# Layer 2's first token group runs its down projection in seven products, and layer 1's activation ends in PSUM

## The chip, the cores and the metric

One core of a Trainium2 chip runs the whole program. The metric is device time in microseconds (us), the median of the runs of one kernel. TensorE is called PE here, VectorE DVE, ScalarE ACT, GpSimd POOL; SP (SyncE) issues the DMAs.

## The reference

Attention with rotary embedding over 4 x 8 heads of 576 tokens and 64 features, then two feed-forward layers over 2304 tokens, d_model 512 and d_ff 2048, all in float32:

```python
x = attn_out.transpose(0, 2, 1, 3).reshape(2304, 512)
h = x @ moe_w_in;  x = (h - np.tanh(h)) @ moe_w_out                  # layer 1
h = x @ moe2_w_in; out = (h / (1.0 + np.exp(-1.702 * h))) @ moe2_w_out   # layer 2
```

The inputs of the two layers come as raw 8-byte words of which the kernel makes float32 weights.

## The kernel before

**Precision.** A float32 product is made of three fast ones: every operand is split into a rounded high part (ACT, a cast) and a low part (value minus high part, POOL or DVE), and high*high, high*low and low*high are added in PSUM.

**Layer 1** has 96 items, one for each of six blocks of 384 tokens and sixteen feature rows of 128 (`item_ops`, `act`, `split`). An item is twelve up matmuls (`up`, L836), the activation, the split of its result, and twelve down matmuls (`down`, L941). The activation g = h - tanh(h) works like this: ACT squares h into z (L901), takes tanh into t (L903), squares z again into u, which lies in PSUM (L906), and makes the mask mk from z (L908). DVE makes w from z and h (L910), subtracts t = h - t (L912), puts a polynomial for small h together in u (L914, L916), and copies u into t where the mask says so (`copy_predicated`, L918). ACT casts t to the high part gh (L926), and POOL makes the low part gl = t - gh (L928), which the down matmuls wait for. h lies in one of the PSUM banks b0 and b1, u in b2, and the raw words that are being converted (`cp`, L325) in b3. w, t, mk and z are SBUF tiles.

Beside the items POOL, ACT and DVE convert weights (`Conv`): the bits (POOL L334, DVE L336), then split parts. For layer 2 they make sums of quarter blocks as well (`conv_in`), split these too (`pieces_of`: ACT L381, POOL L384) and store them to the DRAM tiles w2 (L387). `conv_out` does one word of w_out at a time, without sums.

**Layer 2** takes the six blocks in three pairs (p = 0, 1, 2, the groups) and the sixteen feature rows in eight pairs: 24 steps q (`quad_ops`). A step's up projection is seven products of half-size blocks in place of eight (`product`, L1138, 42 matmuls of 384 columns). The down projection of groups 1 and 2 is seven products too (`down_ops`, `dprod`, L1265): POOL adds and subtracts the four g blocks (L1234 to L1241), seven operands are split (L1397, L1400), 63 matmuls of 256 columns follow, and DVE or ACT adds their results to sums in SBUF (`drain`, L1296 to L1300). The last step of such a group can't be done so and uses `last_down` (L1322, 72 matmuls of 256 columns); then the sums are joined and stored (`close` L1306, `final` L1328, `final_save` L1338). Group 0 runs its down projection plainly (`down2`, L1179, 36 matmuls of 512 columns a step) and meanwhile makes the turned w_out blocks that groups 1 and 2 need (`turn_ops`, ten operations and one store a step, L1198 to L1215).

**What sets the order.** Every operation is given to a planner (`Plan`) with a priority, its cost on each engine that may run it, and the buffers that it uses. The planner lays them out in time and gives each engine a fixed order of instructions; an engine then runs them in that order, each as soon as what it waits for is there. `port=True` tells the planner that an operation on DVE can't run beside POOL; the five DVE operations of layer 1's activation don't carry it. SP issues all DMAs in its own fixed order.

## Time and profile before

| what | us |
|---|---|
| median of 3 runs (1063.17 to 1063.38) | 1063.25 |
| the profiled execution | 1063.46 |
| its span, from the first to the last instruction | 1061.7 |
| PE busy with matmuls | 1038.3 (98%) |
| DVE busy | 693.8 (65%) |
| ACT busy | 719.7 (68%) |
| POOL busy | 780.1 (73%) |
| granted TensorE clock, mean | 0.999 |

Attention lasts to 282 us, layer 1 to 681, the three groups of layer 2 to 805, 926 and the end. A matmul's record is longer than the time it adds to PE, since matmuls overlap: twelve of 384 columns take 2.08 us. So the time from a run of matmuls to the same run one step on is the thing to read.

### The profile page before, as it was taken

To read this page: it belongs to the slowest core of one execution; us is meant where nothing else is said; L and a number is where in the kernel's file an instruction comes from. 1 tells how busy PE (TensorE), PEld (TensorE's weight loads), DVE (VectorE), ACT (ScalarE), POOL (GpSimd) and SP (SyncE) were. 2 spreads that over 40 slices of the span, in tenths; PEclk is the share of its full clock that TensorE was granted. 3 is DMA by queue.
4 is the path that set the end of the run, shared out by engine and by line. 5 is a ranking of instruction groups with operands and counts; after the bars stand their busy time and mean duration, and the time that the engine had idled before them with its cause. 6 is when DMAs were issued, how large, how long until landed. Compare 5 with 4: busy or idle time off the path is not lost.

```text
span 1061.7 us, 19352 instructions
## 1 busy us (share of the span) xinstructions
PE 1038.3 (98%) x6578; PEld 998.7 (94%) x6578; DVE 693.8 (65%) x1243; ACT 719.7 (68%) x1623; POOL 780.1 (73%) x667
## 2 busy tenths in 40 slices
PE   5999999999999999999999999999999999999998
PEld 3898899998999999999999999998888999999998
DVE  7899898899787887777677776654121333562335
ACT  5999999989887776667767776743545444544442
POOL 2888899989356669869978868933933779977763
PEclk9999999999999999999999999999999999999999
DMA  8868778768433326655756578487468676777621
GB/s 280 281 237 308 260 277 281 259 224 294 152 99 120 105 96 214 209 193 191 243 189 227 189 259 308 156 308 280 157 221 340 233 291 224 263 283 266 232 99 60
DMA packets 107188, 236.36 MB, mean 223 GB/s; under 512 B 11729, under 2 KB 61137, under 8 KB 100049
## 3 DMA queue, kind: packets, MB, share of 16 engines
q1 hardware_dynamic: 107088, 235.12, 63.8%
q8 instruction: 52, 0.85, 0.3%
q14 instruction: 48, 0.39, 0.1%
HBM read 157.42 MB, written 49.36 MB: 195 GB/s over the span
## 4 chain that ended last, share of the span: by engine, by line
PE 77%; DVE 7%; ACT 5%; POOL 4%; DMA 3%; issue 3%; SPq 1%; DVEq 0%; ACTq 0%; POOLq 0%
PE ps_h L836 18%; PE y L941 18%; PE ps_h L1138 17%; PE y L1265 10%; PE y L1179 6%; DVE mx L567 2%; PE sp L561 2%; DVE el L624 2%; ACT e L573 2%; PE ps_o L640 2%; PE y L1322 2%; POOL qk L484 1%; PE ps_e L598 1%; ACT eh L626 1%; DMA st<-in_moe_w_out_dram 1%
## 5 line engine op out<-in xcount | busy, mean ns | idle before, releaser
L836 PE MATMUL ps_h<-xh,w 128*128 128x384 f32 x768 | 210.8, 336 | 0.2 <-ACT u L906 0.2
L1138 PE MATMUL ps_h<-xo,ws 128*128 128x384 f32 x1008 | 201.3, 341 | 0.0
L941 PE MATMUL y<-gh,w 128*128 128x384 f32 x768 | 195.6, 336 | 0.0
L1138 PEld LDWEIGHTS ps_h<-xo,ws 128*128 128x128 f32 x1008 | 173.5, 188 | 8.1 <-ACT su L1148 2.1
L836 PEld LDWEIGHTS ps_h<-xh,w 128*128 128x128 f32 x768 | 140.1, 188 | 0.7 <-ACT u L906 0.5
L941 PEld LDWEIGHTS y<-gh,w 128*128 128x128 f32 x768 | 139.0, 188 | 0.0
L928 POOL TENSOR_TENSOR gl<-t,gh 128x384 fp32r<-128x384 f32 x96 | 97.8, 1019 | 42.7 <-ACT gh L926 33.9
L941 PE MATMUL y<-gl,w 128*128 128x384 f32 x384 | 129.0, 336 | 0.0
L836 PE MATMUL ps_h<-xl,w 128*128 128x384 f32 x384 | 128.8, 335 | 0.0
L1296 DVE TENSOR_TENSOR sum<-y,sum 128x256 f32<-128x256 f32 (+1 forms) x108 | 54.0, 537 | 112.8 <-PE y L1265 112.8
L561 PE MATMUL sp<-kt,qt 128*128 128x288 f32 x624 | 115.8, 313 | 1.5 <-ACT e L573 0.9
L573 ACT ACTIVATE e<-sp,mx 128x576 f32<-128x576 f32 x144 | 107.5, 747 | 12.8 <-DVE mx L567 11.6
L567 DVE TENSOR_REDUCE mx<-sp 128x1 f32<-128x576 f32 x144 | 107.2, 748 | 4.8 <-PE sp L561 3.2
L624 DVE TENSOR_TENSOR el<-ps_e,eh 128x512 fp32r<-128x512 f32 x144 | 96.5, 684 | 14.3 <-ACT eh L626 13.4
L626 ACT CAST eh<-ps_e 128x512 fp32r<-128x512 f32 (+2 forms) x208 | 101.7, 532 | 4.6 <-PE ps_e L602 2.0
L910 DVE SCALAR_TENSOR_TENSOR w<-z,ps_h 128x384 f32<-128x384 f32 x96 | 52.8, 550 | 78.5 <-ACT t L903 78.2
L926 ACT CAST gh<-t 128x384 fp32r<-128x384 f32 x96 | 49.3, 513 | 70.9 <-DVE t L918 60.7
L561 PEld LDWEIGHTS sp<-kt,qt 128*128 128x128 f32 x624 | 87.9, 189 | 9.1 <-ACT e L573 7.7
L640 PE MATMUL ps_o<-eh,vw 128*128 128x256 f32 (+1 forms) x320 | 91.1, 307 | 3.5 <-DVE el L624 2.6
L1400 POOL TENSOR_TENSOR ex<-t,g2h 128x384 fp32r<-128x384 f32 x72 | 72.2, 1019 | 25.3 <-ACT g2h L1397 25.3
L1265 PE MATMUL y<-ws,g2h 128*128 128x256 f32 x486 | 90.1, 283 | 0.0
L1265 PE MATMUL y<-ws,ex 128*128 128x256 f32 x345 | 80.7, 282 | 0.0
(143 smaller groups left out, 2525.0 us busy)
## 6 DMA issues: line engine op xcount, KB each, us to landing
ws<-w SPq DMA_DIRECT2D x48, 1024.0 KB
w<-part SPq DMA_DIRECT2D x40, 512.0 KB
kt<-qk SPq DMA_DIRECT2D x64, 288.0 KB
ws<-w SPq DMA_DIRECT2D x24, 768.0 KB
qk<-in_qk_dram SPq DMA_DIRECT2D x30, 576.0 KB
st<-in_moe_w_in_dram SPq DMA_DIRECT2D x32, 512.0 KB
st<-in_moe_w_out_dram SPq DMA_DIRECT2D x32, 512.0 KB
qt<-qk SPq DMA_DIRECT2D x64, 144.0 KB
```

Source lines behind the costliest of these rows:

```text
L561: nc.tensor.matmul(sp[:, half, 0:HS], lhsT=w, rhs=m[:, half * HS:(half + 1) * HS], start=(o == 0), stop=(o == len(ops) - 1))
L567: nc.vector.tensor_reduce(mx, st["sp", n, i], axis=AX.XY, op=ALU.max, negate=True)
L573: nc.scalar.activation(e.rearrange("p (a b) -> p a b", a=2), st.pop(("sp", n, i)), AF.Exp, bias=st.pop(("mx", n, i)), accum_out=st["sum", ...
L624: nc.vector.tensor_sub(lo, src, hi.bitcast(F32))
L626: nc.scalar.copy(hi, src)
L640: nc.tensor.matmul(p[:, 0:wd], lhsT=w[:, h, kc].rearrange("p d a -> p (d a)"), rhs=m, start=(o == 0), stop=(o == 8))
L836: nc.tensor.matmul(p, lhsT=wi[:, a, kk, :], rhs=xx[:, kk, :], start=(o == 0), stop=(o == 11))
L928: nc.gpsimd.tensor_sub(gs[i][1], g, gs[i][0].bitcast(F32))
L941: nc.tensor.matmul(y, lhsT=w[:, a, cols], rhs=g, start=first and o == 0, stop=last and o == 2)
L1138: nc.tensor.matmul(hq[q, b], lhsT=wt(lw, k), rhs=x[:, 2 * lx + k], start=n in (1, 7) and c == 0, stop=n in (2, 3, 4) and c == 5, skip_grou ...
L1265: nc.tensor.matmul(y[:, x:x + 256], lhsT=g[:, cols], rhs=ws[q, s][:, a + l, o:o + 256], start=not own and m == 0, stop=m == 2 and (not own ...
L1400: engine().tensor_sub(l, g, h.bitcast(F32))
```

## The change

The first group's down projection also goes through `down_ops`, and `down2`, `turn` and their helpers fall away. The turned blocks of w_out, with their splits, are made in layer 1: `conv_out` converts the two words of a feature pair together, makes four sums of their halves (`turned`) and stores two more split pieces for each of the first seven pairs. The planner's numbers for when the conversions start and how long they may take (`C2`, `CL`) are lowered. The first group's raw operands no longer wait until all of layer 2's weights are stored, and its preparation is placed 10 us earlier; DVE may share it.

For items 30 to 91 (`inside`) the activation ends the other way round: the mask is that of large h, and `copy_predicated` copies t into u where it holds, so that g lies in PSUM. Then ACT casts from there and the low part is an operation of DVE. u may take bank b2 or b3 for these items.

```diff
-C2, CU, CL = 34, 6, 30
+C2, CU, CL = 28, 6, 20
 DL, TU = 9, 10
+IN0, IN1, INS = 30, 92, 1
...
         if u[0] == "u":
-            return BANKS[2:3]
+            return BANKS[2:4] if inside(u[1]) else BANKS[2:3]
...
-    def conv_out(f, prio, urgent, after):
-        c = Conv((1, f), w2_in, w2_out, 1)
-        i = c.word(prio, urgent, after)
-        n, fp = divmod(f, NF // 2)
-        pieces_of(lambda: c.cz, 512, ("out", f), w2[fp][2][:, 2 * n:2 * n + 2], [("z",) + i], urgent + 1, [("cz",) + i])
+    def conv_out(fp, prio, urgent, after):
+        cs = [Conv((1, f), w2_in, w2_out, 1) for f in (fp, fp + FP)]
...
+        def turned(k):
+            if k == 0:
+                ot[X] = pools["mx"].tile([128, 2, 256], F32, tag="sx", name="sx", bufs=1)
+            x, e = ot[X], engine()
+            if k == 0:
+                e.tensor_sub(x[:, 0], a(0, 1), a(0, 0))
+            elif k == 1:
+                e.tensor_sub(x[:, 1], a(1, 1), a(0, 1))
+            elif k == 2:
+                e.tensor_sub(x[:, 0], a(1, 1), x[:, 0])
+            else:
+                e.tensor_sub(x[:, 1], a(1, 0), x[:, 0])
...
+        pieces_of(both, 512, K[0], w2[fp][3][:, 0:2], S[0:2], t, [X])
...
+        pieces_of(both, 512, K[1], w2[fp][3][:, 2:4], S[2:4], t, [X])
...
+    def inside(i):
+        return IN0 <= i < IN1 and i % INS == 0
...
+        elif k == 3 and inside(i):
+            nc.scalar.activation(mk, z, AF.Relu, bias=-G_T2)
         elif k == 3:
             nc.scalar.activation(mk, z, AF.Relu, scale=-1.0, bias=G_T2)
...
+        elif inside(i):
+            nc.vector.copy_predicated(gt[i][4], mk.bitcast(I32), t)
+            gt[i] = gt[i][4]
         else:
             nc.vector.copy_predicated(t, mk.bitcast(I32), gt[i][4])
             gt[i] = t
...
-            nc.gpsimd.tensor_sub(gs[i][1], g, gs[i][0].bitcast(F32))
+            engine().tensor_sub(gs[i][1], g, gs[i][0].bitcast(F32))
...
+        G = Uu if inside(i) else A
+        low = [_cost("DVE", 0.555)] if inside(i) else [_cost("POOL", 1.01)]
+        op(t + 5, lambda: split(i, 0), [_cost("ACT", 0.515)], [("g", i)], [("gh", i)], [G, GH, GL])
+        op(t + 5.5, lambda: split(i, 1), low, [("g", i), ("gh", i)], [("gl", i)], [G, GH, GL])
...
     def twisted(q):
-        return q >= FP and q % FP < FP - 1
+        return q % FP < FP - 1
...
-        t = T2(FP * p) - (5, 30, 18)[p]
+        t = T2(FP * p) - (15, 30, 18)[p]
...
-               + ([("h0", FP * p - 5)] if p else made), [("raw", p, h)],
+               + ([("h0", FP * p - 5)] if p else []), [("raw", p, h)],
...
-        add = [_cost("POOL", 1.86)] + []
+        add = [_cost("POOL", 1.86)] + ([_cost("DVE", 0.95)] if p == 0 else [])
...
-    def down2(q, u, c):
...
-    def turn(q, k):
...
-    def turn_ops(q):
...
-                   [("w2", "out", f) for f in (fp, fp + FP)] if s == 2 else [("w2", "tt", fp)])
+                   [("w2", "out", f) for f in (fp, fp + FP)] if s == 2 else [("w2", "turned", fp, r) for r in range(2)])
```

The order of DVE around layer 1's item 53, before (w, t, u are the activation's tiles, cz a word under conversion):

```order
L918 COPY_PREDICATED t_7264<-mk_7265,u_7276 128x384
L336 SCALAR_TENSOR_TENSOR cz_7300<-cp_7297,cz_7300 128x512
L910 SCALAR_TENSOR_TENSOR w_7327<-z_7324,ps_h_7284 128x384
L912 TENSOR_TENSOR t_7325<-ps_h_7284,t_7325 128x384
L914 SCALAR_TENSOR_TENSOR u_7337<-u_7337,z_7324 128x384
L916 SCALAR_TENSOR_TENSOR u_7337<-u_7337,w_7327 128x384
L918 COPY_PREDICATED t_7325<-mk_7326,u_7337 128x384
L336 SCALAR_TENSOR_TENSOR cz_7347<-cp_7345,cz_7347 128x512
```

And after, around the same item (L964 is now the predicated copy, L977 the low part):

```order
L956 SCALAR_TENSOR_TENSOR w_7422<-z_7419,ps_h_7389 128x384
L977 TENSOR_TENSOR gl_7437<-u_7402,gh_7436 128x384
L958 TENSOR_TENSOR t_7420<-ps_h_7389,t_7420 128x384
L960 SCALAR_TENSOR_TENSOR u_7441<-u_7441,z_7419 128x384
L962 SCALAR_TENSOR_TENSOR u_7441<-u_7441,w_7422 128x384
L964 COPY_PREDICATED u_7441<-mk_7421,t_7420 128x384
L977 TENSOR_TENSOR gl_7477<-u_7441,gh_7476 128x384
L956 SCALAR_TENSOR_TENSOR w_7485<-z_7482,ps_h_7449 128x384
```

Each item has a sixth operation on DVE, the low part. In 33 of the 62 items it stands right behind the copy, as for u_7441; in others one or more operations of the next item, or a word's, lie between, as w_7422 for u_7402. On ACT the cast to gh stands behind the next item's square in 38 of the 62 items, ahead of it in 24; before it stood behind it in 17.

The order of POOL over one pair's conversion in layer 1, before (sx sums, part split pieces, x and xl the next block's operands):

```order
L384 TENSOR_TENSOR part_7363<-cz_7300,part_7363 128x512
L928 TENSOR_TENSOR gl_7372<-t_7325,gh_7371 128x384
L409 TENSOR_TENSOR sx_7395<-cz_7347 128x256
L384 TENSOR_TENSOR part_7402<-cz_7347,part_7402 128x256
L411 TENSOR_TENSOR sx_7395<-sx_7395,cz_7300 128x256
L872 TENSOR_TENSOR x_7251<-x_7251 128x384
L928 TENSOR_TENSOR gl_7425<-t_7379,gh_7424 128x384
```

And after, at the two words of w_out that follow:

```order
L459 TENSOR_TENSOR sx_7584<-cz_7534 128x256
L338 TENSOR_SCALAR cz_7632<-st_7532 128x512
L461 TENSOR_TENSOR sx_7584<-cz_7632,cz_7534 128x256
L388 TENSOR_TENSOR part_7643<-cz_7632,part_7643 128x512
L388 TENSOR_TENSOR part_7687<-sx_7584,part_7687 128x512
L463 TENSOR_TENSOR sx_7584<-cz_7632,sx_7584 128x256
L465 TENSOR_TENSOR sx_7584<-cz_7632,sx_7584 128x256
L388 TENSOR_TENSOR part_7741<-sx_7584,part_7741 128x512
```

POOL's low parts (L928) are gone from items 30 to 91, and four sums and two low parts of split pieces stand in for every pair. 195 operations lie between the last low part before these items and the first behind them.

The order of PE within a step of the first group, before (ps_h up products, y down sums):

```order
L1138 MATMUL ps_h_10201<-xo_9531,ws_9873 128x384 x6
L1179 MATMUL y_9674<-ws_9890,g2h_10184 128x512 x2
L1179 MATMUL y_9674<-ws_9890,g2l_10185 128x512
L1138 MATMUL ps_h_10249<-xo_9330,ws_10010 128x384 x6
L1179 MATMUL y_9707<-ws_9890,g2h_10184 128x512 x2
L1179 MATMUL y_9707<-ws_9890,g2l_10185 128x512
```

And after:

```order
L1189 MATMUL ps_h_10423<-xo_9626,ws_10032 128x384 x6
L1189 MATMUL ps_h_10507<-xo_9164,ws_10187 128x384 x6
L1255 MATMUL y_10520<-ws_10121,g2h_10430 128x256 x2
L1255 MATMUL y_10520<-ws_10121,ex_9745 128x256
L1189 MATMUL ps_h_10507<-xo_9171,ws_10187 128x384 x6
L1189 MATMUL ps_h_10524<-xo_9379,ws_10187 128x384 x6
L1255 MATMUL y_9721<-ws_10140,g2h_10454 128x256 x2
L1255 MATMUL y_9721<-ws_10140,ex_9745 128x256
```

The up products stand as they stood; in between are runs of three matmuls of 256 columns, 21 of them a step, in place of twelve runs of three of 512. Where the first group gives way to the second, the first sums of the second (DVE and ACT) wait on the landing of the first group's stores, and PE has 27 matmuls that need none of these sums between the last `last_down` run and the next product that needs a free bank.

## Rows read from the trace of the kernel before

**Rows 1.** Busy us (instructions) of PE, PEld, DVE, ACT, POOL by stretch; clock, DMA.

```profile
282.00:681.00 399.00, 398.76 (x2300) 398.22 (x2299) 297.32 (x556) 291.10 (x651) 308.97 (x316) 1.00 0.56 184
400.00:640.00 240.00, 240.00 (x1383) 240.00 (x1382) 174.04 (x325) 172.92 (x392) 197.51 (x210) 1.00 0.65 215
```

**Rows 2.** Waits: PE in layer 1, and DVE from 400 to 640 us (total, times, longest).

```profile
PE ps_h L836 <- ACT u L906: 0.2, 1, 0.2
...
DVE w L910 <- ACT t L903: 53.3, 43, 2.3
```

**Rows 3.** The chain that ended last: start us, us, what, matmuls in the run.

```profile
711.95 2.10 PE ps_h L1138 x12
...
720.84 2.80 PE y L1179 x12
727.87 2.10 PE ps_h L1138 x12
...
834.13 2.09 PE ps_h L1138 x12
...
844.96 4.31 PE y L1265 x36
849.27 2.10 PE ps_h L1138 x12
...
882.71 2.32 PE ps_h L1138 x12
...
913.43 2.12 PE ps_h L1138 x12
...
1048.62 7.59 PE y L1322 x63
```

**Rows 4.** Timeline of one item of layer 1: start us, us, engine, line, operation.

```profile
455.60 0.56 DVE L910 SCALAR_TENSOR_TENSOR w<-z,ps_h 128x384 f32<-128x384 f32 x1 [0.85 <-ACT t L903]
...
457.80 0.59 DVE L918 COPY_PREDICATED t<-mk,u 128x384 f32<-128x384 int32 x1
458.48 0.51 ACT L926 CAST gh<-t 128x384 fp32r<-128x384 f32 x1 [1.27 <-DVE t L918]
...
459.07 1.01 POOL L928 TENSOR_TENSOR gl<-t,gh 128x384 fp32r<-128x384 f32 x1 [0.88 <-ACT gh L926]
...
459.80 0.55 DVE L910 SCALAR_TENSOR_TENSOR w<-z,ps_h 128x384 f32<-128x384 f32 x1 [1.41 <-ACT t L903]
...
462.31 0.51 PE L941 MATMUL y<-gh,w 128*128 128x384 f32 x2
```

**Rows 5.** Groups by line and shape, whole span: count, busy us, mean ns, idle before.

```profile
L384 POOL TENSOR_TENSOR part<-sx,part 128x512 fp32r<-128x512 f32 x16 | 20.8, 1299 | 5.2 <-ACT part L381 4.5
...
L413 POOL TENSOR_TENSOR sx<-cz 128x256 f32<-128x256 f32 x8 | 5.9, 739 | 0.5
...
L334 POOL TENSOR_SCALAR cz<-st 128x512 int32<-128x512 uint8 x64 | 42.2, 659 | 6.4 <-DMA st<-in_moe_w_in_dram 0.9 <-DMA st<-in_moe_w_out_dram 0.3
...
L336 DVE SCALAR_TENSOR_TENSOR cz<-cp,cz 128x512 int32<-128x512 int32 x64 | 43.5, 680 | 9.2 <-POOL cz L334 7.5 <-ACT cp L325 0.8 <-ACT gh L926 0.6
...
L1078 POOL TENSOR_TENSOR x<-raw 128x768 f32<-128x768 f32 x1 | 1.9, 1858 | 0.0
```

**Rows 6.** Two lines of layer 1: count, duration ns min/median/max, first and last start.

```profile
L918 DVE COPY_PREDICATED t<-mk,u x96: 583/601/616, 287.6 to 683.3; 128x384 f32<-128x384 int32 x96
...
L928 POOL TENSOR_TENSOR gl<-t,gh x96: 1007/1017/1058, 288.8 to 685.4; 128x384 fp32r<-128x384 f32 x96
```

**Rows 7.** DVE additions of two SBUF tiles: groups 926 to 936 and 1048 to 1053; timeline.

```profile
L1306 DVE TENSOR_TENSOR sum<-sum 128x256 f32<-128x256 f32 x3 | 4.5, 1506 | 0.0
...
L1306 DVE TENSOR_TENSOR sum<-sum 128x256 f32<-128x256 f32 x5 | 2.1, 415 | 0.0
...
708.22 1.02 POOL L1167 TENSOR_TENSOR g2l<-t,g2h 128x384 fp32r<-128x384 f32 x1 [1.02 <-ACT g2h L1165]
708.26 1.25 DVE L1200 TENSOR_TENSOR tt<-tt 128x256 f32<-128x256 f32 x1
```

More of the change, by code (lines that the diff above doesn't have):

```diff
@@ L1167, in split2 @@
             nc.gpsimd.tensor_sub(gs[q, u][1], g, gs[q, u][0].bitcast(F32))
-    def down2(q, u, c):
-        p, fp = divmod(q, FP)
-        n, j = divmod(u, 2)
-        gh, gl = gs[q, u]
-        cols = slice(c * 128, (c + 1) * 128)
-        first, last = fp == 0 and n == 0, fp == FP - 1 and n == 1
-        if first:
-            acc["2", p, j, c] = bank(("y2", p, j, c), "y")
-        y = acc["2", p, j, c]
-        for o, (a, g) in enumerate(((0, gh), (1, gh), (0, gl))):
-            nc.tensor.matmul(y, lhsT=g[:, cols], rhs=ws[q, 2][:, 2 * n + a, :], start=first and o == 0, stop=last and o == 2)
@@ L1382, in down_ops @@
         if fp == 0:
-            free = [("h0", q)] + ([("end", p - 1, 0, d, c, n) for d in range(2) for c in range(3) for n in range(2)] if p > 1 else [])
+            free = [("h0", q)] + ([("end", p - 1, 0, d, c, n) for d in range(2) for c in range(3) for n in range(2)] if p else [])
             for n in (0, 2, 3, 4):
```

111 lines of the change are left out of this document (38 added, 73 removed).

## The prediction

> **What bounds the kernel now.** I read the busy time by stretch first, then the waits, then the chain that ended last, then one item's timeline. TensorE (PE) is busy for 398.8 of layer 1's 399 us, at the full granted clock of 1.00 (2.4 GHz) [rows 1], and waited 0.2 us in it [rows 2]; the chain of the whole second half runs over matmuls, run after run [rows 3]. So a stage lasts as long as its matmuls, and only what changes PE's own work, or makes PE wait, moves the time. In layer 1 an item (24 matmuls of 384 columns) takes 4.16 us, 399 / 96 [rows 1]. In layer 2 one step of the first group takes 15.92 us, and one step of the second, which already has the seven products, 15.14: the reader compares the same run of 12 matmuls, one step on [rows 3].
>
> The engines beside PE are not idle in layer 1. From 400 to 640 us VectorE is busy 174 of 240 us and GpSimd 197.5 [rows 1]. What matters is that VectorE's free time is mostly not free: of its 66 idle us it spent 53.3 waiting for ScalarE's tanh of the next item [rows 2]. One item shows the loop [rows 4]: w starts at 455.60 and the fifth operation, the predicated copy, ends at 458.39; then ScalarE rounds g (458.48), squares the next h and takes its tanh, and VectorE's next w, released by that tanh, starts at 459.80. That is 4.20 us a turn, against the 4.16 that PE needs. The margin is a stock, not a rate: GpSimd's low part ends at 460.08, the down product that reads it starts at 462.31, so 2.2 us are in hand.
>
> **The change, part by part.**
>
> *Seven products in the first group.* Seven steps lose 36 matmuls of 512 columns (2.80 us for 12, so 8.40 a step) and get 63 of 256 (4.31 for 36, so 7.54) [rows 3]: 7 x 0.86 = 6.0 us less work. By whole steps, with their small gaps, it is 7 x (15.92 - 15.14) = 5.5; I take this one. The group's last step loses 8.40 and gets 72 matmuls at 7.59/63 = 0.120 [rows 3], 8.67: +0.3. Two steps of the second group, where GpSimd also makes the next group's operands, took 15.36 each (882.71 to 913.43) [rows 3]; the first group will now look like that: +0.4. Together -4.8.
>
> *The border between the groups.* The first group now keeps its sums in the tiles (st, cz) that the second group wants too, so the second group's first sums, on ScalarE and VectorE, wait until the first's results are stored; behind them on VectorE stand the next up product's additions. No row shows this wait. The price lies between nothing (the order puts 27 matmuls there that need no sum) and the 4.2 us that the kernel's end takes from its last matmul run to the landing of its last store (from 1048.62 + 7.59, 1056.2, to the span's end at 1061.7 are 5.5, of which 1.3 are PE's own last matmuls) [rows 3], less 27 matmuls at 0.17: near nothing again. I take +0.5, and -4.3 in all for layer 2.
>
> *What leaves layer 2.* Seven times ten operations that turn w_out, and seven stores of 1 MB, go; each step loads 1.75 MB for the down product in place of 1. PE did not stand still behind any of these, so they cost and give nothing; the second group runs its 15.14 us with the same loads [rows 3]. If that cover went, PE would wait for ws at a step's head.
>
> *What comes into layer 1.* GpSimd loses 62 low parts of 1.02 us (63) [rows 6] and gets 28 sums of 0.74 and 14 low parts of 1.30 (39) [rows 5]. Between the low parts that frame the 62 items its queue has 195 operations; with the durations of their kinds (1.30, 0.74, 0.66, 1.02, and 1.86 for seven early operand steps) [rows 5, 6] that is 190 us of 62 x 4.16 = 258, a share of 0.74. ScalarE gets 14 roundings, some 9 us in 258, and SP 14 stores of 0.5 MB; ScalarE's 67 free us in 240 and a DMA share of 0.65 [rows 1] hide them, and by the order the last conversion stands some ten items ahead of layer 2. The bank b3 is now shared by u and the conversion: u is held from ScalarE's square to VectorE's low part, about 4.3 us in 8.3, and four conversions of some 1.8 us come in 25: two banks two thirds taken. Nothing, as long as VectorE is on time.
>
> *VectorE's queue in layer 1.* This decides. Per item it has 2.79 us from w to the end of the copy, plus the low part at 0.53 (0.55 as the same operation on h and tanh, less the overlap) [rows 4]: 62 x 3.32 = 205.8. Thirty conversion words at 0.62 (0.68 less the overlap) [rows 5] (18.6) and four sums (2.2) stand in the same stretch. In 33 items the order puts the low part right behind the copy, so VectorE stands still while ScalarE rounds: 0.62 each (from 458.39 to 459.07, as GpSimd waited before [rows 4]), 20.5; eight more lose about 0.15. Sum 248 of 258 us. So far PE is not held up.
>
> But the copy itself changes its operands. Before, it wrote t in SBUF from the mask in SBUF and u in PSUM; now it writes u in PSUM from the mask and t, **both in SBUF**. Before, no operation of the item read two SBUF tiles, and none ever waited for GpSimd: 96 copies lie between 583 and 616 ns, 96 low parts of GpSimd between 1007 and 1058 [rows 6]. Where VectorE does read two SBUF tiles beside a running GpSimd operation, the trace shows it held until that one is nearly over: an addition of 256 columns that takes 0.415 us where GpSimd rests (five near the kernel's end) took 1.25 from 708.26 on, with GpSimd's operation running from 708.22 to 709.24, and three between 926 and 936 us, beside a busy GpSimd, averaged 1.5 [rows 7]. So the wait is what is left of GpSimd's operation, less 0.14 us (0.98 left, 0.84 waited). For a copy that comes at any moment: half the mean operation, weighted by length, is 0.53 us; (0.53 - 0.14) x 0.74 = 0.29 us a copy. 62 copies: 18 us. 248 + 18 = 266 against 258: 8.3 over, less the 2.2 in hand: 6.1. In some dozen items, where ScalarE takes the next square only behind the rounding, the loop is the 4.20 of above rather than the 3.92 counted: +0.28 each, 3.4. So between 6.1 and 9.5; I take 7.5. The bounds: no wait at all (the nearest rows are the copies as they were [rows 6]), and 0.5 us a copy (the whole weighted half, GpSimd never idle): 31 us, 21 over after the stock, less what GpSimd's lighter last items give back, some 16.
>
> The Trainium skill, SBUF — State Buffer, section "Who interferes with whom", speaks against the change: a VectorE instruction with two SBUF inputs is blocked by a GpSimd instruction that reads SBUF until that one has ended, one with a single SBUF input is not. No run here shows it for a predicated copy; for additions the trace agrees. Taken whole, without the 0.14, the rule gives 0.53 x 0.74 = 0.39 us a copy, 24 us in place of 18, and 1072 in place of the sum below.
>
> **Sum.** The profiled execution took 1063.46 us, 1061.7 of it the span; the median of the runs is 1063.25, so changes of the span are added to the median. 1063.25 - 4.3 + 7.5 = 1066.4.
>
> **Rivals.**
>
> *The copy does not wait (chance 0.30; faster).* The mask may not count as a second tile, or the waits fall into the time in which VectorE waits for tanh anyway. For: 53 us of such waits [rows 2] and a planned load of 248 in 258. Against: the low part is put into just that time. Then 1063.25 - 4.3 = 1058.9, between 1057.7 (whole work of 6.0, no border) and 1061.
>
> *Half of it (0.26; within 0.2%).* Port waits are there, but the orders in which ScalarE takes the next square ahead of the rounding (38 of 62 items) catch up: PE loses 2.2 to 6.4 us, 1061.1 to 1065.4, the middle 1063.2. The border wait of up to 4 us on top of the first rival also ends here.
>
> *The forecast (0.44; slower).* PE loses more than 6.4 us: 1065.4 to 1075. It decides as soon as the copy's mean passes 0.60 + 0.28 us.
>
> That the change does not do what it says has no chance worth a number: the order shows the 63 products and the low parts on VectorE.
>
> **How the numbers follow.** A measurement of this kernel tells 0.2%, 2.1 us, from no change. The three cases are the three signs: faster 0.30, same 0.26, slower 0.44. The range leaves out the first rival's lowest corner and the forecast's top, together a little under 0.2: 1058.0 to 1072.0. The forecast's own range is 1065.4 to 1072.
>
> **What would show it.** In the profile after: the first group's steps at 15.1 to 15.4 us and no matmuls of 512 columns (layer 2's part); the border without a gap over 0.5 us; the copies between item 30 and 91 with a mean near 0.9 us and single ones over 1.2, GpSimd's operations longer beside them; PE with waits for the low part in layer 1, and layer 1 longer than 399 us by the loss. Copies still at 0.60 us would make the forecast wrong, and the time would be near 1059; copies at 0.9 with layer 1 unchanged would say that the stock and the catching up were worth more than I gave them.

## The result: slower by 1.3%, and the profile after

The changed kernel takes 1076.62 us (median of five runs, 1076.08 to 1080.24) against 1063.38 before: a ratio of 1.0131, 95% interval 1.0111 to 1.0152. The forecast was 1066.4, range 1058.0 to 1072.0: the direction was right, the size a quarter of what came, and the range too low at its upper end. The profiled execution took 1079.52 us, its span 1077.7; it is 2.9 us above the median; 2.7 of that are two stretches in which the granted clock was lower, shown below.

The line of the copy moved: what was L918 [rows 6] is L964 in the 62 items whose low part VectorE takes, and L967 in the others; the low part is L977, the up matmuls are L877, the down matmuls L990, layer 2's products L1189 and its seven down products L1255.

To cut the time in two, I take layer 1 from its first up matmul to the end of its last down matmul; in all kernels here the same matmuls stand around that point. First and last rows before, by the timeline of TensorE (start us, us, engine, line, operation):

```profile
281.87 0.43 PE L836 MATMUL ps_h<-xh,w 128*128 128x384 f32 x1
...
688.43 0.34 PE L941 MATMUL y<-gl,w 128*128 128x384 f32 x1
```

And after:

```profile
282.74 0.43 PE L877 MATMUL ps_h<-xh,w 128*128 128x384 f32 x1
...
708.71 0.34 PE L990 MATMUL y<-gl,w 128*128 128x384 f32 x1
```

Layer 1 took 688.8 - 281.9 = 406.9 us before and 709.0 - 282.7 = 426.3 after: **+19.4**. What follows it to the end of the span took 1061.7 - 688.8 = 372.9 before and 1077.7 - 709.0 = 368.7 after: **-4.2**. The rest (+0.9) is ahead of layer 1, in a stretch near 25 us at a granted clock of 0.83, and 1.8 of the 19.4 are the clock too. By stretch (columns as in [rows 1]):

```profile
400.00:640.00 240.00, 232.84 (x1303) 226.90 (x1301) 201.90 (x352) 167.14 (x378) 182.67 (x188) 0.99 0.65 222
...
570.00:580.00 10.00, 7.86 (x37) 7.54 (x36) 8.00 (x15) 8.47 (x20) 9.27 (x10) 0.83 0.69 242
```

TensorE, busy 240.0 of these 240 us before, is busy 232.8. VectorE went from 174.0 to 201.9, GpSimd from 197.5 to 182.7. Who TensorE waited for from 282 to 715 us, the four largest sums (total, times, longest):

```profile
PE y L990 <- DVE gl L977: 4.1, 5, 1.8
PE y L990 <- ACT yo L1002: 3.9, 3, 2.1
PE y L990 <- ACT gh L975: 1.4, 2, 0.7
PE ps_h L1189 <- ACT t L1210: 1.3, 1, 1.3
```

The last of the four is behind layer 1. Before, the one such wait was 0.2 us [rows 2]. All waits listed for layer 1 sum to some 11 us, less than its loss. A wait is listed from the end of the record ahead, and that record, 0.34 us, is longer than the 0.17 us from one matmul's start to the next; delays too short to be listed make up what is left. The copies and the low parts, by group over layer 1 (count, busy us, mean ns, idle before):

```profile
L964 DVE COPY_PREDICATED u<-mk,t 128x384 f32<-128x384 int32 x62 | 55.3, 892 | 4.3
L977 DVE TENSOR_TENSOR gl<-u,gh 128x384 fp32r<-128x384 f32 x62 | 34.4, 555 | 22.1 <-ACT gh L975 21.4
```

And the line of the copies (shortest, median and longest in ns, first and last start):

```profile
L964 DVE COPY_PREDICATED u<-mk,t x62: 556/824/2283, 412.5 to 687.4; 128x384 f32<-128x384 int32 x62
```

The copies that ran from 583 to 616 ns [rows 6] now run from 556 to 2283. One of them in full, VectorE and GpSimd around 450 us:

```profile
450.33 1.03 DVE L964 COPY_PREDICATED u<-mk,t 128x384 f32<-128x384 int32 x1
...
449.65 1.30 POOL L388 TENSOR_TENSOR part<-cz,part 128x512 fp32r<-128x512 f32 x1 [0.99 <-ACT part L385]
```

GpSimd's operation had 0.62 us left when the copy began (449.65 + 1.30 - 450.33), and the copy took 0.47 longer than its 0.56: the rest less 0.15, close to the 0.14 that the prediction drew from the additions in [rows 7]. It holds for the whole line: 40 of the 62 copies are longer than 0.63 us, and each of the 40 is longer than the shortest copy by what was left of GpSimd's operation, less 0.128 to 0.139 us. The other 22 found GpSimd idle or with under 0.2 us left, or began with it or ahead of it. The longest one, and what it set off:

```profile
671.84 2.28 DVE L964 COPY_PREDICATED u<-mk,t 128x384 f32<-128x384 int32 x1
671.84 1.86 POOL L1146 TENSOR_TENSOR xo<-x,xo 128x768 fp32r<-128x768 f32 x1
...
674.04 2.58 DVE L1146 TENSOR_TENSOR xo<-raw,xo 128x768 fp32r<-128x768 f32 x1
...
674.16 0.48 ACT L975 CAST gh<-u 128x384 fp32r<-128x384 f32 x1 [3.01 <-DVE u L964]
...
677.15 0.44 PE L990 MATMUL y<-gl,w 128*128 128x384 f32 x1 [1.79 <-DVE gl L977]
```

The copy starts together with a long step of layer 2's first operands and waits for all of it; ScalarE stands 3.01 us; VectorE, whose next instruction is such an operand step itself, is held by GpSimd's next operation (from 673.77, 2.04 us) and takes 2.58 us for it; then comes the low part, and TensorE has stood 1.79 us. It works in the other direction too: a GpSimd operation that starts while a copy runs is held. L388 took 1.65 us at 602.44, in place of 1.30, beside a copy from 602.37 to 602.94.

Layer 2 came out as forecast in its sum. The chain that ended last, one step of the first group to the next:

```profile
729.16 2.11 PE ps_h L1189 x12
...
744.21 2.09 PE ps_h L1189 x12
```

15.05 us a step in place of the 15.92 of [rows 3]. Two waits that I had not foreseen stand against that. One is the load of ScalarE's table for layer 2's activation, which before lay under other work of TensorE (684.48 to 685.76, TensorE busy throughout):

```profile
709.58 1.28 ACT L1210 ACT_TABLE_LOAD   x1
...
711.42 1.85 PE L1189 MATMUL ps_h<-xo,ws 128*128 128x384 f32 x9 [1.31 <-ACT t L1210]
```

The other is GpSimd's queue in the seventh step: three operand steps of the second group stand ahead of the mixes that the down products need, and ScalarE, which waits for a mix, holds up a copy of sums behind it.

```profile
808.33 1.84 POOL L1146 TENSOR_TENSOR xo<-x,xo 128x768 fp32r<-128x768 f32 x1
...
810.13 1.01 POOL L1224 TENSOR_TENSOR t<-t 128x384 f32<-128x384 f32 x1
```

(The two ahead of the first row start at 804.74 and 806.53.) TensorE's next product starts at 813.21, 1.2 us after the matmul ahead of it. At the border between the groups, for which I had put 0.5, no wait is seen.

### The profile page after: what moved, and what is told of

Same layout as the page of the kernel before. It is cut to its first block, busy times and chain, and to the rows that moved or that the text cites. A ratio compares the mean times of both kernels' runs of the same rounds, so it can differ in the third digit from the quotient of the medians.

```text
span 1077.7 us, 20007 instructions
## 1 busy us (share of the span) xinstructions
PE 1040.9 (97%) x6803; PEld 1006.8 (93%) x6803; DVE 752.7 (70%) x1341; ACT 726.0 (67%) x1643; POOL 801.7 (74%) x685
## 4 chain that ended last, share of the span: by engine, by line
PE 53%; DVE 19%; ACT 11%; POOL 7%; issue 6%; DMA 3%; SPq 1%; DVEq 0%; ACTq 0%; POOLq 0%
PE ps_h L1189 15%; PE y L1255 14%; PE ps_h L877 7%; PE y L990 7%; PE sp L602 3%; DVE u L964 3%; ACT e L614 3%; DVE mx L608 2%; PE y L1312 2%; PE ps_o L681 2%; DVE u L962 2%; DVE el L665 2%; DVE u L960 2%; ACT eh L667 2%; PE ps_e L639 2%
## 5 line engine op out<-in xcount | busy, mean ns | idle before, releaser
L877 PE MATMUL ps_h<-xh,w 128*128 128x384 f32 x768 | 212.7, 338 | 1.3 <-DVE t L958 1.1
L1189 PE MATMUL ps_h<-xo,ws 128*128 128x384 f32 x1008 | 200.3, 341 | 2.8 <-ACT t L1210 1.3
L990 PE MATMUL y<-gh,w 128*128 128x384 f32 x768 | 196.8, 337 | 5.3 <-ACT yo L1002 3.9
L1286 DVE TENSOR_TENSOR sum<-y,sum 128x512 f32<-128x512 f32 (+1 forms) x162 | 81.3, 538 | 163.7 <-PE y L1255 159.9
L1189 PEld LDWEIGHTS ps_h<-xo,ws 128*128 128x128 f32 x1008 | 171.0, 188 | 6.6 <-ACT t L1210 1.6
L1390 POOL TENSOR_TENSOR ex<-t,g2h 128x384 fp32r<-128x384 f32 x132 | 132.3, 1021 | 34.3 <-ACT g2h L1387 34.2
L990 PEld LDWEIGHTS y<-gh,w 128*128 128x128 f32 x768 | 138.4, 188 | 7.5 <-ACT yo L1002 4.9
L1255 PE MATMUL y<-ws,g2h 128*128 128x256 f32 x792 | 144.9, 281 | 0.0
L877 PEld LDWEIGHTS ps_h<-xh,w 128*128 128x128 f32 x768 | 141.1, 189 | 2.5 <-DVE t L958 1.8
L990 PE MATMUL y<-gl,w 128*128 128x384 f32 x384 | 130.8, 341 | 4.7 <-DVE gl L977 4.1
L877 PE MATMUL ps_h<-xl,w 128*128 128x384 f32 x384 | 129.5, 337 | 0.0
L1255 PE MATMUL y<-ws,ex 128*128 128x256 f32 x492 | 126.8, 280 | 0.0
L1255 PEld LDWEIGHTS y<-ws,g2h 128*128 128x128 f32 x792 | 126.2, 188 | 0.3 <-DVE sum L1286 0.2
L665 DVE TENSOR_TENSOR el<-ps_e,eh 128x512 fp32r<-128x512 f32 x144 | 96.6, 685 | 14.3 <-ACT eh L667 13.2
L1255 PEld LDWEIGHTS y<-ws,ex 128*128 128x128 f32 x492 | 89.1, 188 | 0.0
L1387 ACT CAST g2h<-t 128x384 fp32r<-128x384 f32 x132 | 67.3, 514 | 27.6 <-POOL t L1224 11.4
```

The source lines that it names most:

```text
L665: nc.vector.tensor_sub(lo, src, hi.bitcast(F32))
L877: nc.tensor.matmul(p, lhsT=wi[:, a, kk, :], rhs=xx[:, kk, :], start=(o == 0), stop=(o == 11))
L990: nc.tensor.matmul(y, lhsT=w[:, a, cols], rhs=g, start=first and o == 0, stop=last and o == 2)
L1189: nc.tensor.matmul(hq[q, b], lhsT=wt(lw, k), rhs=x[:, 2 * lx + k], start=n in (1, 7) and c == 0, stop=n in (2, 3, 4) and c == 5, skip_grou ...
L1255: nc.tensor.matmul(y[:, x:x + 256], lhsT=g[:, cols], rhs=ws[q, s][:, a + l, o:o + 256], start=not own and m == 0, stop=m == 2 and (not own ...
L1286: nc.vector.tensor_add(s, y, s)
```

## The experiments

Theory 1: the copy, with two SBUF inputs, waits for GpSimd, and these waits are the loss in layer 1. Theory 2: VectorE's longer queue and its order lose the time, wait or no wait. All kernels are built from the changed kernel but for e4, e12 and e14, which are built from the one before. The kernel's planner lays down the order of every queue, so that an edit to a cost or a tile moves other instructions as well; where the order stayed the same, it is said. Medians, ratios to the kernel before in the same series, and the two parts of the profiled execution (cut as above):

| kernel | median us | ratio (95%) | layer 1 | rest |
|---|---|---|---|---|
| before | 1063.38 | | 406.9 | 372.9 |
| after | 1076.62 | 1.0131 (1.0111 to 1.0152) | 426.3 | 368.7 |
| e1 copy from h's bank | 1067.65 | 1.0033 (1.0022 to 1.0044) | 415.1 | 369.0 |
| e2 copy as before | 1071.67 | 1.0074 (1.0058 to 1.0089) | 420.6 | 368.8 |
| e3 layer 2's part alone | 1091.27 | 1.0260 (1.0243 to 1.0278) | 439.5 | 368.7 |
| e4 layer 1's part alone | 1077.48 | 1.0128 (1.0113 to 1.0143) | 422.2 | 372.1 |
| e5 e1, half the items | 1071.47 | 1.0072 (1.0057 to 1.0087) | 418.3 | 368.9 |
| e6 e1, two waits of layer 2 out | 1067.89 | 1.0038 (1.0023 to 1.0053) | 416.3 | 366.5 |
| e7 e5 and e6 | 1071.41 | 1.0075 (1.0060 to 1.0090) | 420.9 | 366.5 |
| e8 e6, not at ends of blocks | 1075.61 | 1.0115 (1.0098 to 1.0132) | 425.4 | 366.2 |
| e9 planner knows of the wait | 1065.41 | 1.0014 (1.0005 to 1.0023) | 411.7 | 369.5 |
| e10 e6, seven planner numbers | 1058.90 | 0.9953 (0.9940 to 0.9965) | 410.8 | 363.9 |
| e11 e10, t back in SBUF | 1073.94 | 1.0093 (1.0077 to 1.0108) | 426.0 | 364.2 |
| e12 before, two planner numbers | 1062.18 | 0.9986 (0.9977 to 0.9995) | 407.0 | 371.2 |
| e13 e10 without a small tile | 1056.10 | 0.9929 (0.9917 to 0.9942) | 407.5 | 365.0 |
| e14 before with that tile | 1064.23 | 1.0008 (0.9999 to 1.0017) | 410.5 | 370.5 |

**e1, one SBUF input at the copy.** The subtraction h - tanh(h) writes over h in PSUM, and the copy takes it from there:

```
-            nc.vector.tensor_sub(t, p, t)
+            nc.vector.tensor_sub(p if inside(i) else t, p, t)
...
-            nc.vector.copy_predicated(gt[i][4], mk.bitcast(I32), t)
+            nc.vector.copy_predicated(gt[i][4], mk.bitcast(I32), p)
...
-        a(8, 3.4, _cost("DVE", 0.593), [("m", i), ("t", i), ("u", i)], [("g", i)], [Uu] + D)
+        a(8, 3.4, _cost("DVE", 0.593), [("m", i), ("t", i), ("u", i)], [("g", i)], [Uu] + D + ([H] if inside(i) else []))
```

> The changed kernel, with one operand moved: in the 62 items whose low part is on VectorE, t = h - tanh(h) is written over h in its PSUM bank, and the predicated copy takes it from there, so that it reads one SBUF tile (the mask) in place of two. Theory 1, the copy waits for GpSimd because both its inputs lie in SBUF: the copies fall from a mean of 0.89 us to 0.57 to 0.62, single ones over 1 us go, TensorE loses under 4 us between 400 and 712 us in place of 20, and the time is 1058 to 1063 us. Theory 2, VectorE's longer queue and the order in it (low parts behind ScalarE's rounding, conversion words, the shared bank b3) cost the time: the copies shorten, since 0.3 us each is seen in the trace, but layer 1 still loses over 10 us and the time is 1069 us or more.

The line of the copies in e1:

```profile
L964 DVE COPY_PREDICATED u<-mk,ps_h x62: 551/562/564, 411.6 to 674.3; 128x384 f32<-128x384 int32 x62
```

And TensorE's largest sum of waits in layer 1:

```profile
PE ps_h L877 <- DVE u L964: 3.9, 5, 2.5
```

No copy waits any more: 551 to 564 ns for all 62, beside the same kinds of work on GpSimd. That is the two-input wait, gone with one operand; the planner's order moved with it, and e11 below leaves the order alone. But the time fell between the two theories: 9 of the 13 us went, and layer 1 still loses 8.2. This rest is not VectorE's queue alone, as theory 2 would have it. The wait shown is for h's bank, which this edit holds longer, from the subtraction to the copy. The longest of the five, on VectorE and TensorE:

```profile
630.42 0.56 DVE L958 TENSOR_TENSOR ps_h<-ps_h,t 128x384 f32<-128x384 f32 x1
...
632.95 0.55 DVE L964 COPY_PREDICATED u<-mk,ps_h 128x384 f32<-128x384 int32 x1
...
633.56 0.69 PE L877 MATMUL ps_h<-xh,w 128*128 128x384 f32 x1 [2.52 <-DVE u L964]
```

In the changed kernel the bank would have been free at 630.98, before this wait began; the same is so of the other four, and 1.6 us of the 8.2 are a stretch at a lower clock behind this one. How much of the 8.2 would stand without the longer hold, as a wait for a low part, is not shown.

**e2, the copy as before, the low part on VectorE.** The copy writes t in SBUF again from u; then the low part reads two SBUF tiles:

```
-            return BANKS[2:4] if inside(u[1]) else BANKS[2:3]
+            return BANKS[2:3]
...
-        elif inside(i):
-            nc.vector.copy_predicated(gt[i][4], mk.bitcast(I32), t)
-            gt[i] = gt[i][4]
```

> The changed kernel, but the activation ends in SBUF as before (the copy writes t from the mask and u, u only in bank b2), and VectorE still takes the low part of items 30 to 91, now from t and gh, both in SBUF. Theory 1 (two SBUF inputs wait): the wait goes over to the low parts, whose mean rises from 0.56 to 0.8 to 0.95 us, the copies are at 0.60, and the time stays within 6 us of the changed kernel's 1076.6. Theory 2, as far as it is the bank b3 that u shares with the conversions: that sharing is gone, and the time falls under 1068 us.

The copies and the low parts of e2, by group:

```profile
L962 DVE COPY_PREDICATED t<-mk,u 128x384 f32<-128x384 int32 x96 | 57.6, 600 | 7.2
L972 DVE TENSOR_TENSOR gl<-t,gh 128x384 fp32r<-128x384 f32 x62 | 50.4, 812 | 28.0 <-ACT gh L970 27.4
```

The wait moved as theory 1 said: copies at 600 ns, low parts at 812 in place of 555. The time is 5 us below the changed kernel's, within the 6 I had allowed, and above the 1068 of theory 2. The waits, some 16 us in sum for 20, cost less here. A likely reason, not tested by itself: behind the copy stands ScalarE's rounding, and behind that the low part; behind the low part, on VectorE, only the next operation.

**e3, layer 2's part alone.** `IN0, IN1, INS = 0, 0, 1`: GpSimd makes all low parts and the new sums.

> The changed kernel without its part in layer 1's activation (no item has its low part on VectorE; GpSimd takes all 96 low parts besides the new sums). This shows layer 2's part alone. Layer 2, from its first product to the end, keeps the 2.6 us that the changed kernel gains there. GpSimd has some 253 us of work in the 258 of items 30 to 91. If it keeps up, the time is 1060 to 1062 us; if its queue falls behind, TensorE waits for low parts and the time is 1064 to 1075 us. The copies are at 0.60 us in both.

What TensorE waited for most:

```profile
PE y L990 <- POOL gl L977: 16.9, 7, 6.7
```

Well over both expectations: +27 us. I had counted 253 us of GpSimd's work in 258, and taken "almost full" for "loses a few". The waits are for GpSimd's low parts, 6.7 us the longest. So the low parts had to leave GpSimd; the question was only where to and in which form. Layer 2 keeps its 4.2.

**e4, layer 1's part alone**, on the kernel before: the lines `inside`, the mask's sign, the copy into u, the low part on VectorE and the bank b3 for u, as in the change; layer 2 and its weights as before.

> The kernel before, with the activation's part of the change alone (items 30 to 91 end in PSUM, VectorE takes their low part), layer 2 and its weights as before. Theory 1: GpSimd is idle more often here (its share falls from 0.82 to about 0.56), so the copies wait less, a mean of 0.75 to 0.85 us, and layer 1 loses 4 to 10 us: 1067 to 1073 us in all. Theory 2: the same number of low parts behind ScalarE, so layer 1 loses as much as in the changed kernel, 16 us, and the time is near 1079 us. If GpSimd's new sums were needed for any loss, the time is 1062 to 1064 us.

The copies by group, and the stretch from 400 to 640 us:

```profile
L924 DVE COPY_PREDICATED u<-mk,t 128x384 f32<-128x384 int32 x62 | 53.5, 863 | 5.5
```

```profile
400.00:640.00 240.00, 234.66 (x1324) 232.56 (x1323) 206.37 (x361) 162.67 (x372) 145.47 (x148) 0.99 0.59 197
```

GpSimd is busy 145 of 240 us in place of 183, and the copies wait nearly as much: 863 ns against 892. A lighter GpSimd does not free the copy in proportion, as I had expected (0.75 to 0.85), and the time is near that of theory 2. Since the copies wait as much, this run does not tell the two theories apart. Layer 1's part alone costs all of the loss, 13.4 us; the new sums are not needed for it.

**e5, half the items** (`INS = 2`, on e1).

> The kernel of e1 (the copy reads one SBUF tile), but only every second item of 30 to 91 has its low part on VectorE: 31 in place of 62. VectorE gets 31 x 0.555 = 17 us less work there, and 31 low parts and roundings fewer stand behind each other; GpSimd gets 31 x 1.02 = 32 us more, 222 us in 258. Theory: what is left of e1's loss in layer 1 (PE waits of 6 us there, mostly where a block of 16 items ends) is VectorE's queue, which has no time to catch up; then TensorE loses under 3 us between 400 and 695 us and the time is 1061 to 1064 us. Rival: GpSimd's queue, which has the new sums, is as near its limit as VectorE's; then low parts on GpSimd end the waits of TensorE and the time is 1068 us or more.

Slower than e1 by 4 us, against the theory; but the rival's sign is weak too: TensorE's waits for low parts of GpSimd are 1.6 us, the others still end with VectorE (`PE ps_h L877 <- DVE u L964` 5.8). From 400 to 640 us VectorE has 15 us less work than in e1 (179.0 for 193.9) and GpSimd 26 more (202.7 for 176.7), and it is worse. Through which wait the one delays the other these runs don't settle.

**e6, two waits of layer 2** (on e1). A one-column activation loads the table behind the last mask of layer 1; VectorE may take additions of the second group's operands:

```
+    tabt = const.tile([128, 1], F32, name="tabt")
+
+    def preload():
+        nc.scalar.activation(tabt, ident[:, 0:1], AF.Gelu_apprx_sigmoid)
...
+        if i == n1 - 1:
+            op(t + 2.41, preload, [("ACT", 1.4, 1.5)], [("m", i)], [("tab",)])
...
-        add = [_cost("POOL", 1.86)] + ([_cost("DVE", 0.95)] if p == 0 else [])
+        add = [_cost("POOL", 1.86)] + ([_cost("DVE", 0.95)] if p < 2 else [])
```

> The kernel of e1 with two edits for layer 2: ScalarE loads its table for layer 2's activation right behind layer 1's last mask, by an activation of one column (in the changed kernel the load of 1.28 us stood ahead of the first activation of layer 2, and TensorE waited 1.3 us for it); and VectorE may take additions of the second group's operands (before, GpSimd alone, whose queue held a step of the first group up, 1.5 us of TensorE's time). Expected if these two waits are worth what the trace shows: 1.3 and 1.5 us less than e1, 1064 to 1066 us, and no wait of TensorE over 0.6 us between 690 and 830 us. Rival: the time goes to the next engine in the chain and comes back as another wait; then the time stays at e1's 1067.6 within 1 us.

Both waits went: from 690 to 830 us TensorE's one listed wait is `PE y L1262 <- DVE sum L1293` at 0.3 us, and the rest after layer 1 is 2.5 us shorter than in e1. The median is not: layer 1 is longer, 416.3 us for 415.1, though e1's has 1.6 us of a lower clock in it. The likely reason came with e13: e6 has the tile `tabt`, and its matmuls in layer 1 start 0.1753 us apart, in e1 0.1738, which is 3.5 us over 2304 matmuls.

**e7 and e8.** e7 is e5 and e6 together; e8 is e6 with `and i % 16 not in (14, 15, 0, 1)` in `inside`.

> e5 and e6 together: one SBUF input at the copy, every second item inside, the table loaded early, VectorE taking part in the second group's operands. If the terms add, layer 1 loses under 3 us and layer 2 gains 5 to 6 against the kernel before: 1058 to 1062 us, faster than the kernel before. If GpSimd's queue becomes the bound with 31 low parts more, 1065 us or more.

> e6, but the items at the ends of blocks (the last two and the first two of each sixteen) keep their low part on GpSimd, 46 of the 62 stay on VectorE. e1's waits of TensorE in layer 1 stand where a block ends and ScalarE copies four sums out besides. If it is these places alone, layer 1 loses under 3 us and the time is 1059 to 1063 us; if it is VectorE's queue over the whole stretch, the waits move to other items and the time stays near e6's.

Both expectations missed: 1071.41 and 1075.61. Giving 31 low parts back to GpSimd costs 3.5 us against e6, giving back 16 at the ends of blocks 7.7. In e8 TensorE's waits still stand near the ends of blocks (from 497 to 501, 559 to 576 and at 647 us), but 4.7 us of them, the largest sum, are now for low parts of GpSimd. So in e8's order neither queue had room for the other's work there; in e7 the waits are spread over more items.

**e9, the planner knows of the wait.** Same operands as the changed kernel; the planner, which keeps operations marked `port` apart from GpSimd's, is told that the copy is one:

```
-        a(8, 3.4, _cost("DVE", 0.593), [("m", i), ("t", i), ("u", i)], [("g", i)], [Uu] + D)
+        a(8, 3.4, _cost("DVE", 0.593), [("m", i), ("t", i), ("u", i)], [("g", i)], [Uu] + D, port=inside(i))
```

> The changed kernel, instruction for instruction the same kinds and operands (the copy keeps its two SBUF inputs), but the planner is told that the copy and GpSimd's operations exclude each other, as it is told for the other operations of VectorE with two SBUF tiles; so only the order differs. Theory: half of the loss is that the order was made for copies of 0.60 us, so that what was planned behind each other slid apart; with an order that knows of the wait, copies still average 0.75 us or more, but the time falls to 1066 to 1070 us. Rival: the waits cost the same in any order, since VectorE's queue is full: 1074 us or more.

The copies by group:

```profile
L964 DVE COPY_PREDICATED u<-mk,t 128x384 f32<-128x384 int32 x62 | 47.4, 767 | 1.7
```

11.2 us of the 13.2 back by order alone (one addition of layer 2's first operands moved from GpSimd to VectorE with it), a little more than expected, with copies that still wait, though less (767 ns for 892). VectorE's waits for the rounding fall too, from 18.3 us in 30 to 11.7 in 15 between 400 and 640 us.

**e10 and e11, a better order, and the operand by itself.** e10 is e6 with other numbers in the planner:

```
-CS, CP, X1 = -0.5, 13.2, 30
+CS, CP, X1 = -0.5, 12, 30
...
-C2, CU, CL = 28, 6, 20
-DL, TU = 9, 10
-IN0, IN1, INS = 30, 92, 1
+C2, CU, CL = 26, 6, 28
+DL, TU = 9.5, 10
+IN0, IN1, INS = 26, 92, 1
...
-    UR = 14.7
+    UR = 14.4
...
-        t = T2(FP * p) - (15, 30, 18)[p]
+        t = T2(FP * p) - (15, 40, 18)[p]
```

> e6 (one SBUF input at the copy, early table load, VectorE in the second group's operands) with seven numbers of the planner changed: the conversions of layer 2's weights start at item 26 in place of 28 and are due later (28 items of slack in place of 20), items 26 to 91 are inside, the second group's operands are made earlier, and three due times of layer 1's conversions and layer 2's steps move by little. Theory: what e6 still loses in layer 1 (waits at the ends of blocks, 2.6 us the longest) is a matter of order, and VectorE's and GpSimd's queues have just room enough; then no wait of TensorE over 0.6 us is left, layer 1 takes 399 to 401 us, layer 2 keeps its gain of 5 to 6, and the time is 1057 to 1061 us, faster than the kernel before. Rival: VectorE's queue is full in any order: 1065 us or more.

e11 puts t back in SBUF, and nothing else: the four engines have the same instructions in the same order.

> e10, in the same order on every engine, with one operand put back: t stays in SBUF, so that the copy reads two SBUF tiles as in the changed kernel. Theory: the copies go from 0.57 back to 0.85 to 0.95 us, VectorE's queue in layer 1 has no room for 66 such waits (some 20 us), and the time is 8 to 14 us above e10's. Rival: in a better order the waits fall where VectorE would have waited for ScalarE anyway; then it is within 3 us of e10's.

e10, the stretch from 400 to 640 us and all of TensorE's waits in layer 1:

```profile
400.00:640.00 240.00, 240.00 (x1371) 239.91 (x1370) 197.14 (x377) 172.83 (x392) 164.84 (x178) 1.00 0.65 218
```

```profile
PE ps_h L877 <- DVE t L958: 0.2, 1, 0.2
```

e11, the copies by group, and the waits:

```profile
L964 DVE COPY_PREDICATED u<-mk,t 128x384 f32<-128x384 int32 x66 | 59.7, 905 | 4.1
```

```profile
PE y L990 <- DVE gl L977: 2.6, 6, 1.0
PE y L990 <- ACT yo L1002: 2.4, 2, 1.9
PE y L990 <- ACT gh L975: 2.4, 5, 0.9
```

This is the cleanest pair: one operand's place, 15.0 us. 66 copies wait 0.905 - 0.562 = 0.34 us each, 22.6 us in sum, and two thirds of it become time, in an order that without them has but the 0.2 us shown. (A stretch at a granted clock of 0.83, from 495 to 505 us, stands behind one of e11's waits and counts in its time.) VectorE is busy 197 of 240 us in e10, with 24.1 us of waits for ScalarE's rounding besides: room was there for the work, not for the waits.

**e12, how much of e10 is order of layer 2 alone.** `DL = 9.5` and `UR = 14.4` in the kernel before.

> The kernel before with the two numbers of e10 that set the order of layer 2's steps (the down products of a step due 9.5 in place of 9 us after their operands, steps of the second and third group planned 14.4 us apart in place of 14.7), and nothing else. It tells how much of e10's gain needs none of the change. In e10 the steps take 14.9 us, in e6 15.0 to 15.1, with the same matmuls. Theory: that difference comes from this order; the second and third group have 14 such steps, so this kernel is 2 to 4 us faster than the kernel before, 1060 to 1062 us, and some two thirds of e10's gain is order alone. Rival: the shorter steps need the freed queues; then the time is within 1 us of the kernel before.

1.3 us, under the theory's 2 to 4, of the 5.0 that e10 gains. The other planner numbers were not tried on the kernel before, so that how much of the remaining 3.7 needs the change, and how much a better order would give without it, stays open.

**e13 and e14, a tile of one column.** What remained was e6, and with it layer 1 of e10: no wait over 0.2 us, and yet 3.9 us longer than before. e13 is e10 without the tile `tabt` (the activation writes over a column of the identity, which is not read any more), in the same order:

```
-    tabt = const.tile([128, 1], F32, name="tabt")
...
-        nc.scalar.activation(tabt, ident[:, 0:1], AF.Gelu_apprx_sigmoid)
+        nc.scalar.activation(ident[:, 0:1], ident[:, 0:1], AF.Gelu_apprx_sigmoid)
```

> e10 without the one-column tile that its early table load writes to (the activation writes over a column of the identity, which layer 1 and 2 don't read); everything else, the order too, as in e10. In e6, e10 and e11, which have that tile, a matmul of 384 columns in layer 1 starts 0.1753 us after the one ahead of it, in all kernels without it 0.1736 to 0.1744, with no wait between them. Theory: the tile moves all tiles behind it in SBUF by a few bytes and so the pace of layer 1's 2304 matmuls; without it layer 1 is 3 to 4.5 us shorter and the time is 1054.5 to 1056.5 us. Rival: the pace comes from the order or the load beside it; then the time stays within 1 us of 1058.9.

The chain in layer 1 (start us, us, what, matmuls in the run), in e10 and then in e13:

```profile
451.33 2.12 PE y L990 x12
453.45 2.12 PE ps_h L877 x12
```

```profile
441.08 2.10 PE y L990 x12
443.19 2.09 PE ps_h L877 x12
```

e14 is the kernel before with `pad = const.tile([128, 1], F32, name="pad")` and one memset of it.

> The kernel before with one unused tile of one column behind the identity (set to zero once, at the start) and nothing else. If the place of the tiles in SBUF sets the matmuls' pace, layer 1 goes from 0.1737 to 0.175 us a matmul and the time rises by 2 to 4.5 us, to 1066 to 1068 us. If not, it is within 1 us of the kernel before.

The chain in e14:

```profile
450.39 2.12 PE y L943 x12
452.51 2.12 PE ps_h L838 x12
...
723.44 2.75 PE y L1181 x12
```

The lines show the longer runs of twelve; not all are. In layer 1 of e14 112 of 166 runs take 2.12 us and 51 take 2.08; in the kernel before one takes 2.12, 120 take 2.08 and the others mostly 2.09 or 2.10. e10 and e13 differ in the same way. Layer 1 takes 3.6 us more in e14, as expected of the pace; the time rises by 0.6 only, against my 2 to 4.5, since the rest is 2.4 us shorter: layer 2's down matmuls run faster, twelve of 512 columns in 2.73 to 2.76 us in place of 2.74 to 2.81, and those of 256 columns start 0.1195 us apart in place of 0.1208. e13 takes 1056.10 us: it beats the kernel before by 0.7% (ratio 0.9929, 0.9917 to 0.9942), and the changed one by 20 us.

## Why the prediction was right in its sign and wrong in its size

*Layer 2, forecast -4.3.* It gave 4.2 (372.9 to 368.7). The steps took 15.05 us, not 15.14. The last quads' crowding, put at +0.4, was the wait of 1.2 us that follows GpSimd's operand steps; the load of the table, 1.3 us, was not in the sum; the border, put at 0.5, cost nothing visible. The terms as measured (7 x 0.87 less, 0.3, 1.2 and 1.3 more) give 3.3; the 0.9 that is left is mostly in the third group, put at nothing: from its first product to the end are 134.6 us in place of 135.3. The errors cancelled to a tenth; the sum was right partly by luck. e6 confirms the two waits by taking them out: the rest went from 369.0 to 366.5.

*The copy's wait, forecast 0.29 us for 62 copies, 18 us.* Measured 0.33 (0.892 less the 0.562 of e1), 20.5 us; singles lay far over 1.2 us, as was asked of the trace. That it comes from the second SBUF input is shown by e1 and, in an unchanged order, by e11 against e10. The Trainium skill, SBUF — State Buffer, section "Who interferes with whom", has this rule in terms of SBUF inputs; the trace agrees for the predicated copy, with the mask counting as an input: with mask and data in SBUF it waits (0.892), with the mask alone (0.562) it doesn't. Taken whole the rule gave 0.39 us a copy, mine 0.29; the measured 0.33 lies between. Here too two errors made up for each other: 40 of 62 copies were held, 0.65 and not 0.74, and each of these waited 0.51 us and not 0.39.

*"248 + 18 = 266 against 258: 8.3 over, less the 2.2 in hand: 6.1".* This is the step that failed, from the waits to the loss: the term of +7.5 measured 17.6 besides the clock, though the waits were put at 18 and came to 20.5. A sum over 62 items treats the stretch as one pool of time, in which VectorE's free 10 us take up waits wherever they fall. The runs show otherwise. In e11, against e10 in the same order, 15.0 of 22.6 us of waits became time, though VectorE was idle for 43 of 240 us in e10. And how much becomes time hangs on the order, which the sum does not have: in e9, whose order was made for the wait, 12.7 us of waits (62 times 0.767 less 0.562) left layer 1 only 4.8 us longer.

*"Sum 248 of 258 us. So far PE is not held up."* This stays half open. e1, which has the queue and none of the wait, loses 8.2 us in layer 1, not zero, but most of its waits stand at the bank that its own edit holds longer. In the order of e10 and e13, where VectorE's work and its waits for the rounding fill 221 of 240 us (e10), the queue costs next to nothing: layer 1 takes 407.5 us in e13, 406.9 before. Of VectorE's 240 us from 400 on, 201.9 were work, and the waits listed for it in the trace were mostly two:

```profile
DVE gl L977 <- ACT gh L975: 18.3, 30, 1.1
DVE w L956 <- ACT t L947: 6.5, 19, 0.7
```

The first is the wait of the low part for the rounding, the 20.5 us of the prediction, and right. Why VectorE's free time takes up so little I read from these two rows, and no run isolates it: both waits end with ScalarE, so each stands in a loop. When VectorE is late, ScalarE's tanh is late, and the next item begins late. The 2.2 us in hand are spent once, and by the sum the queue has 10 us in 258 to win them back.

*The parts of the 17.6.* With 10 us free I let 10 of the 18 vanish. e1's layer 1 lost 6.6 us besides the clock, so that 11.0 of the 17.6 went with the wait; what the 6.6 are is open, as said.

*The first rival, "the copy does not wait", 1058.9.* As priced it was wrong for the same reason: in the order that the planner gave, e1 took 1067.65. With a better order it is right for layer 1: no copy waits in e13, and its layer 1 takes 407.5 us, before 406.9. That e10's 1058.90 is the very number of the rival is chance: e10's layer 1 is 3.9 us longer, 3.3 of it by the tile, and its rest is 9.0 shorter, by more than the rival's 4.3. *The second, half of it, with orders that catch up:* the planner's order was made for copies of 0.59 us. e9 shows that an order made for the wait gets back 11 of 13 us. Both cause and cure lie in the pair of the operand and the order, and either alone repairs most of it.

*GpSimd, forecast a share of 0.74.* 182.7 of 240 is 0.76. Right; and e3 shows what that part was worth: with those low parts on GpSimd the loss is 27 us.

*The clock.* TensorE's timeline in the stretch whose granted clock averaged 0.83 (part of it at 1.2 GHz, the rest at 2.4):

```profile
574.11 0.86 PE L990 MATMUL y<-gh,w 128*128 128x384 f32 x2 [2.15 <-ACT yo L1002]
574.77 0.52 PE L990 MATMUL y<-gl,w 128*128 128x384 f32 x1
575.09 0.52 PE L877 MATMUL ps_h<-xh,w 128*128 128x384 f32 x1
```

After a wait of 2.15 us twelve matmuls start 0.32 us apart in place of 0.17. That is the 1.8 us above. The waits that ended at 641.70 and 677.15 (1.55 and 1.79 us) had nothing of the kind behind them, and three of the five runs had a mean granted clock of 1.00.

What stays open: why e4's copies wait as much beside a GpSimd that works a fifth less. From 412 to 688 us GpSimd is busy 161 of 276 us in e4, a share of 0.58, and 39 of the 62 copies are longer than 0.63 us, 0.63; in the changed kernel it is busy 198, a share of 0.72, and 40 are longer, 0.65. So e4's copies met GpSimd about as often as its share says, and the changed kernel's less often. That copies and GpSimd's operations are released by the same events would fit, but it was not tried.

## What to carry to other kernels

Before moving an operation to VectorE, count the SBUF inputs of every operation whose operands move with it, masks included: here one operand kept in PSUM was worth 15 us in 1074. A queue that is 92% full by such a sum, as e10's, may hold its work in a good order, but don't set new waits against the idle time that the sum leaves: two thirds of e11's became time. Give the planner the wait, since order alone was worth 11 us. And where a matmul-bound stage changes length without a wait, compare the start-to-start time of its matmuls before looking for a cause in the change.

## What the runs showed that I had not expected

- One tile of one column ahead of the others in SBUF changed the pace of matmuls without any wait: two thirds of layer 1's runs of twelve took 2.12 us in place of 2.08 to 2.10, and layer 2's down matmuls got faster (e14). Over 400 us of layer 1 that is 3.6 us. The tiles' place in SBUF is what the edit moves, besides one memset at the start, so it is the likely cause; no run here tells which tile or which address matters.
- The wait between VectorE and GpSimd goes both ways: GpSimd's operation of 1.30 us took 1.65 when it began beside a running copy. The one that is held waits until 0.13 us before the other's end (40 copies).
- A predicated copy with its mask in SBUF and its data in PSUM, written to PSUM, takes 0.562 us; the same with its data in SBUF takes 0.556 at its shortest. The second input costs nothing when GpSimd rests.
